# Where g and four chunks of w_out lie in SBUF, and second-product matmuls of 256 columns in four blocks

## The chip, the cores and the metric

The kernel runs on one core of a Trainium2 chip. The metric is device time in microseconds (us) of one execution. Before the change three runs took 1107.73, 1110.91 and 1111.5 us, median 1110.91 us. One execution was profiled: it took 1110.88 us, of which 1109.1 us is the span from the first to the last instruction; the remaining 1.8 us lies around it.

## The reference

Two stages, joined by a transpose. First, linear attention with an exponential feature map, for 8 batches, 8 heads, 576 positions and head dimension 64:

```python
proj = x @ w_phi                                   # for q and for k, 128 features
proj = proj - max(abs(proj), axis=-1)
phi = concat([exp(proj), exp(-proj)])              # 256 features
kv = einsum('bhsf,bhsd->bhfd', k_p, v); z = sum(k_p, axis=2)
attn = einsum('bhsf,bhfd->bhsd', q_p, kv) / (einsum('bhsf,bhf->bhs', q_p, z) + 1e-6)
```

Then a feed-forward layer on all 4608 tokens (512 model columns, 2048 hidden ones):

```python
x = attn.transpose(0, 2, 1, 3).reshape(4608, 512)
h = x @ w_in                                       # 512 -> 2048
g = 0.5 * h * (1 + erf(h / sqrt(2)))
out = g @ w_out                                    # 2048 -> 512
```

`w_in` and `w_out` are of type float64 here, handed to the kernel as 64-bit words.

## The kernel before

The feed-forward part is what the change touches. It goes through the tokens in 18 blocks of 256 (`TB`). To keep precision, each factor is split into a high and a low float32r part, and a product is three matmuls: high by high, and the two mixed ones. In `block(j, ...)`:

- The first product fills `ph`, 128 hidden columns at a time. For each of the 16 hidden chunks `f` it takes 12 matmuls: 4 chunks of the model dimension by three pairs of parts. Each has a 128x128 piece of `w_in` (tile `w_i`) as the stationary operand and 256 tokens of `xh` or `xl` as the moving one.
- ScalarE applies Gelu twice, once into `gh` (the high part, written as float32r) and once in place, and VectorE subtracts to get `gl`. Each tile holds two chunks of 256 tokens, so a unit `u` is two hidden chunks.
- The second product adds into `po`, [128, 2, 512]. For each hidden chunk it takes 6 matmuls: two halves `m` of the tokens by three pairs of parts (`gh` with both parts of `w_out`, `gl` with the high one). The stationary operand is a 128x128 piece of `gh` or `gl`, the moving one is a row of 512 columns of `w_o{f}`, the split tile of hidden chunk `f`. A block has 96 of these. Where the next thing on TensorE is a first product, the last matmul of the second product's unit is already cut in two halves of 256 columns (`cut`); in the last unit it is the one before the last.

Every matmul has its own load of the stationary operand (PEld in the profile).

The attention of the 8 batches runs interleaved with the first blocks. All operations are recorded by `op(...)` with a cost, a rank and the buffers that they read and write. `Plan.order` sorts them by rank and by when buffers come free in its own cost model, and `Plan.emit` writes them out in that order; from then on each engine follows its own fixed sequence. The tiles `gh` and `gl` have two buffers each.

Where a tile lies is settled when the program is built. `place(...)` reserves tiles in order at the start: `kvn`, the sixteen `w_o`, `gh`, `gl`, the sixteen `w_i`, `dc`, `xh`, `xl`. Addresses are bytes within a partition. In the program before, all of `w_o`, `gh`, `gl` and `w_i` start at a multiple of 256, and so do all the pieces that matmuls read of them, since the pieces are 512 or 2048 bytes apart. The moving tiles `xh` and `xl` start at 192 modulo 256, as do `kt` and `ek` of the attention; `wst` starts at 128; the buffers of `kvn` start at 128, 160, 192 and 224.

In the attention, `pk` is the projection of keys (a 128-column piece of `kt` is stationary, `wst` is moving), `pq` that of queries (`wst` is stationary), `kv` the sum over positions and `pn` the numerator (64 columns of `kvn` are stationary, `ef` is moving). Its operands are plain float32 and each of its matmuls leaves two records in the trace.

Of the kernel before, what the change touches and what calls it, by code (L numbers as in the profile page):

```python
# [10 lines left out]
F32 = mybir.dt.float32  # L11
F32R = mybir.dt.float32r
# [15 lines left out]
P = 128  # L28
# [4 lines left out]
NFC = DFF // P  # L33
SHIFT = 1e-6
KC = 9


class Buf:
# [215 lines left out]
def mm_cost(m, n):  # L254
    return (n / 2.286 + 3.0) / 1e3
# [6 lines left out]
def dve(n, psum=False, fast=False):  # L262
    return ((62 if psum else 66) + (n / 2 if fast else n)) / 960


def act(n, psum=False):
    return (n / 1.2 + (51 if psum else 93)) / 1e3
# [15 lines left out]
def fused_kernel(ctx: ExitStack, tc: tile.TileContext, qT, kT, va, w_st, w_in, w_out, out):  # L283
# [17 lines left out]
    def mm(*a, **kw):  # L301
        return tc.keep_in_program_order(nc.tensor.matmul(*a, **kw))  # L302


    def place(tag, shape, dt=F32):
        spool.tile(shape, dt, tag=tag, name=f"place_{tag}", bufs=SLOTS.get(tag, 1))

    place("kvn", [P, 4, D + 1])
    for f in range(NFC):
        place(f"w_o{f}", [P, 2, 512])  # L310
    place("gh", [P, 2, TB])
    place("gl", [P, 2, TB])
    for q in (2, 0, 3, 1):
        for c in range(NCC):
            place(f"w_i{c}_{q}", [P, 2, 512])
# [16 lines left out]
    def copy(eng, cost, dst, src, r, w, **kw):  # L332
        e = {"dve": nc.vector, "pool": nc.gpsimd}.get(eng)
        if eng == "act":
            op(eng, cost, lambda: nc.scalar.copy(out=dst(), in_=src()), r=r, w=w, **kw)  # L335
        else:
            op(eng, cost, lambda: e.tensor_copy(out=dst(), in_=src()), r=r, w=w, **kw)

    def tt(eng, cost, dst, a, b, o, r, w, **kw):
        e = {"dve": nc.vector, "pool": nc.gpsimd}[eng]  # L340
        op(eng, cost, lambda: e.tensor_tensor(out=dst(), in0=a(), in1=b(), op=o), r=r, w=w, **kw)  # L341
# [5 lines left out]
    def split_weight(src, nm, rank):  # L347
        tag = f"w_{nm}"
        raw = plan.pool(spool, tag, 1)([P, 512, 2], U32, f"raw_{nm}")
        w = plan.pool(spool, tag, 1)([P, 2, 512], F32R, f"w_{nm}")  # L350
        t = sb["ob"]([P, 512], U32, f"wt_{nm}")
        k = dict(rank=rank)
        op("sp", 0.06, lambda: nc.sync.dma_start(out=raw().bitcast(I64), in_=src), w=[raw], kb=524, **k)
        low, high = (lambda: raw()[:, :, 0]), (lambda: raw()[:, :, 1])
        v = nc.vector
        op("act", act(512) + 0.04, lambda: nc.scalar.activation(t().bitcast(F32), high().bitcast(F32), AF.Abs), r=[raw], w=[t], **k)
        op("dve", dve(512, fast=True), lambda: v.tensor_scalar(
            out=t().bitcast(F32), in0=t().bitcast(F32), scalar1=F64_MIN, scalar2=F64_MAX, op0=ALU.max, op1=ALU.min), r=[t], w=[t], **k)
        op("dve", dve(512, fast=True), lambda: v.tensor_scalar(
            out=t(), in0=t(), scalar1=3, scalar2=0x3FFFFFF8, op0=ALU.logical_shift_left, op1=ALU.bitwise_and), r=[t], w=[t], **k)  # L360
        op("dve", dve(512), lambda: v.scalar_tensor_tensor(
            out=t(), in0=low(), scalar=29, in1=t(), op0=ALU.logical_shift_right, op1=ALU.bitwise_or), r=[raw, t], w=[t], **k)
        op("dve", dve(512), lambda: v.scalar_tensor_tensor(
            out=t(), in0=high(), scalar=0xC0000000, in1=t(), op0=ALU.bitwise_and, op1=ALU.bitwise_or), r=[raw, t], w=[t], **k)
        hi = lambda: w()[:, 0, :]
        copy("act", act(512), hi, lambda: t().bitcast(F32), [t], [w], **k)
        tt("dve", dve(512), lambda: w()[:, 1, :], lambda: t().bitcast(F32), lambda: hi().bitcast(F32), ALU.subtract, [t, w], [w], **k)
        return w

    wi, wo = {}, {}  # L370

# [180 lines left out]
    def block(j, rank):  # L552
        plan.stream = "f"
        xr = sb["xr"]([P, NCC, TB], F32, f"xr_{j}")
        rb = sb["rb"]([P, NCC, TB], F32, f"rb_{j}")
        xh_all = sb["xh"]([P, NCC * TB], F32R, f"xh_{j}")
        xl_all = sb["xl"]([P, NCC * TB], F32R, f"xl_{j}")
        xh = lambda: xh_all()[:, : NCC * TB].rearrange("p (c t) -> p c t", c=NCC)
        xl = lambda: xl_all()[:, : NCC * TB].rearrange("p (c t) -> p c t", c=NCC)
        t = j * TB  # L560
        while t < (j + 1) * TB:
            b, s = divmod(t, S)
            h, s = divmod(s, HS)
            n = min(HS - s, (j + 1) * TB - t)
            o = t - j * TB
            for c in range(NCC):
                op("sp", 0.06, lambda b=b, c=c, h=h, s=s, n=n, o=o: nc.sync.dma_start(
                    out=xr()[:, c, o : o + n], in_=x_d[b][c][h]()[:, s : s + n]), r=[x_d[b][c][h]], w=[xr], kb=n * 0.512,
                   rank=rank(0) - 8)
            for i in range(2):  # L570
                op("sp", 0.06, lambda b=b, i=i, h=h, s=s, n=n, o=o: nc.sync.dma_start(
                    out=rb()[64 * i : 64 * i + 64, :, o : o + n],
                    in_=r_d[b][h]()[:, s : s + n].rearrange("(c i) t -> i c t", i=2)[i : i + 1].to_broadcast([64, NCC, n])),
                   r=[r_d[b][h]], w=[rb], kb=n * 1.024, rank=rank(0) - 8)
            t += n
        tt("dve", dve(NCC * TB), xr, xr, rb, ALU.mult, [xr, rb], [xr], rank=rank(0) - 4)
        copy("dve", dve(NCC * TB, fast=True), xh, xr, [xr], [xh_all], rank=rank(0) - 4)
        tt("dve", dve(NCC * TB), xl, xr, lambda: xh().bitcast(F32), ALU.subtract, [xr, xh_all], [xl_all], rank=rank(0) - 4)
        po = ps["po"]([P, 2, DM], F32, f"po_{j}")
        for u in range(NU):  # L580
            rk = rank(u / NU)
            ph = ps["ph"]([P, 2, TB], F32, f"ph_{j}_{u}")
            for i in range(2):

                def mm1(ph=ph, u=u, i=i):
                    ins = []
                    f = 2 * u + i
                    fs = slice(f % 4 * P, f % 4 * P + P)
                    for c in range(NCC):
                        for w, x in ((0, xh), (0, xl), (1, xh)):  # L590
                            ins.append(mm(ph()[:, i, :], lhsT=wi[c, f // 4]()[:, w, fs], rhs=x()[:, c, :], start=len(ins) == 0, stop=len(ins) == 11))
                    return ins

                op("pe", 12 * mm_cost(128, TB), mm1, r=[xh_all, xl_all] + [wi[c, u // 2] for c in range(NCC)], w=[ph], rank=rk, part="first")
            gh = sb["gh"]([P, 2, TB], F32R, f"gh_{j}_{u}")
            gl = sb["gl"]([P, 2, TB], F32R, f"gl_{j}_{u}")
            op("act", act(2 * TB, True) + 0.016, lambda gh=gh, ph=ph: nc.scalar.activation(gh(), ph(), AF.Gelu), r=[ph], w=[gh], table="gelu", rank=URGE + rk)  # L597
            op("act", act(2 * TB, True) + 0.037, lambda ph=ph: nc.scalar.activation(ph(), ph(), AF.Gelu), r=[ph], w=[ph], table="gelu", rank=URGE + rk)  # L598
            tt("dve", dve(2 * TB, True), gl, ph, lambda gh=gh: gh().bitcast(F32), ALU.subtract, [ph, gh], [gl], rank=URGE + rk, port=False)
            for i in range(2):  # L600

                def mm2(u=u, i=i, gh=gh, gl=gl):
                    ins = []
                    f = 2 * u + i
                    for m in range(2):
                        ms = slice(m * P, (m + 1) * P)
                        for n, (g, w) in enumerate(((gh, 0), (gh, 1), (gl, 0))):
                            cut = plan.then == "first" and m == 1 and n == (1 if f == NFC - 1 else 2)
                            for cs in (slice(0, DM // 2), slice(DM // 2, DM)) if cut else (slice(0, DM),):
                                ins.append(mm(po()[:, m, cs], lhsT=g()[:, i, ms], rhs=wo[f]()[:, w, cs], start=f == 0 and n == 0,  # L610
                                              stop=f == NFC - 1 and n == 2, skip_group_check=cut))
                    return ins

                op("pe", 6 * mm_cost(128, DM), mm2, r=[gh, gl, wo[2 * u + i]], w=[po], rank=rk)
        for m in range(2):
            ob = sb["ob"]([P, DM], F32, f"ob_{j}_{m}")
            copy("act", act(DM, True), ob, lambda m=m: po()[:, m], [po], [ob], rank=rank(1))
            op("sp", 0.06, lambda m=m, ob=ob: nc.sync.dma_start(out=out[j * TB + m * P : j * TB + (m + 1) * P, :], in_=ob()), r=[ob], kb=262, rank=rank(1))
# [92 lines left out]
```

## Time and profile before

| | |
|---|---|
| three runs | 1107.73, 1110.91, 1111.5 us (median 1110.91) |
| profiled execution | 1110.88 us, span 1109.1 us |
| instructions in the span | 21711 |
| VectorE busy | 475.7 us (43%) |
| ScalarE busy | 567.2 us (51%) |
| GpSimd busy | 315.9 us (28%) |
| DMA | 84.92 MB, mean 77 GB/s |

The page of the profile gives busy time by engine: PE is TensorE's matmuls, PEld its loads of stationary operands, DVE VectorE, ACT ScalarE, POOL GpSimd. A matmul's record covers its way through the array, so the records of consecutive matmuls overlap; the rate at which matmuls follow each other is read from a run of them (its length over their number), not from the mean length of a record. The chain of waits follows the work that ended last back from the last instruction and merges consecutive pieces of one engine and line. The view of stretches gives each engine's busy time, number of instructions and the granted TensorE clock between two times; it counts an instruction that reaches in from outside.

### The profile page before, as it was taken

The page shows a single profiled execution, that of the slowest core. Times are in us where ns is not written, and L with a number is a line of the kernel's source. Part 1 is how long each engine was busy: PE and PEld are TensorE (multiplying, and loading weights), DVE is VectorE, ACT ScalarE, POOL GpSimd, SP SyncE. Part 2 cuts the span into 40 slices and gives each one's busy share as a digit, 9 for nine tenths or more (in the row PEclk, how much of TensorE's full clock was granted, in tenths as well). Part 3 has the DMA queues.
Part 4 walks back from the last instruction along what each step waited for, and adds up shares of the span by engine and source line. Part 5 has one row for each costly group of instructions (what it writes and reads, how often), then busy time and mean ns, then how long its engine had stood idle before and what let it go on. Part 6 is the DMA issues. An engine that isn't in the chain of part 4 may idle for free.

```text
span 1109.1 us, 21711 instructions
## 1 busy us (share of the span) xinstructions
PE 1082.1 (98%) x9183; PEld 908.2 (82%) x9183; DVE 475.7 (43%) x743; ACT 567.2 (51%) x883; POOL 315.9 (28%) x116
## 2 busy tenths in 40 slices
PE   7879999999999999999999999999999999999998
PEld 4547868878878887888778889999999999999997
DVE  5889996364483553544645441212112112212010
ACT  5777786667777667877657642212212121212121
POOL 1330223376564574457556550000000000000000
PEclk8989999999999999999999999999999999999999
DMA  6787533124232332322411202102102012010000
GB/s 248 258 260 207 157 93 96 50 72 117 66 97 63 88 98 56 103 64 67 122 40 48 63 22 58 39 20 58 36 23 58 15 43 58 1 38 20 1 20 20
DMA packets 73938, 84.92 MB, mean 77 GB/s; under 512 B 23968, under 2 KB 60992, under 8 KB 73840
## 3 DMA queue, kind: packets, MB, share of 16 engines
q1 hardware_dynamic: 73840, 83.52, 25.3%
q8 instruction: 72, 1.18, 0.5%
q14 instruction: 26, 0.21, 0.1%
HBM read 64.32 MB, written 19.17 MB: 75 GB/s over the span
## 4 chain that ended last, share of the span: by engine, by line
PE 86%; DVE 6%; ACT 4%; DMA 2%; issue 1%; POOL 1%; ACTq 0%; SPq 0%; POOLq 0%; DVEq 0%
PE po L302 35%; PE ph L302 34%; PE pn L302 6%; PE kv L302 5%; PE pq L302 3%; PE pk L302 3%; ACT ek L430 1%; DVE mx L425 1%; DVE ek L341 1%; ACT ef L479 1%; DMA x_d<-xo 1%; PE spin L302 1%; DMA d_d<-xo 1%; DMA kt<-in_kT_dram 1%; ACT L597 0%
## 5 line engine op out<-in xcount | busy, mean ns | idle before, releaser
L302 PE MATMUL ph<-xh,w_i 128*128 128x256 f32 x2304 | 418.5, 279 | 0.0
L302 PEld LDWEIGHTS ph<-xh,w_i 128*128 128x128 f32 x2304 | 357.2, 188 | 7.9 <-issue 6.3
L302 PE MATMUL po<-w_o,gh 128*128 128x512 f32 (+1 forms) x1168 | 363.6, 394 | 0.0
L302 PE MATMUL ph<-xl,w_i 128*128 128x256 f32 x1152 | 319.2, 277 | 0.0
L341 DVE TENSOR_TENSOR gl<-ph,gh 128x512 fp32r<-128x512 f32 x144 | 99.2, 689 | 415.8 <-ACT ph L598 413.4
L302 PEld LDWEIGHTS po<-w_o,gh 128*128 128x128 f32 x1168 | 211.3, 188 | 49.7 <-issue 6.0
L597 ACT ACTIVATE gh<-ph 128x512 fp32r<-128x512 f32 x144 | 86.1, 598 | 298.9 <-PE ph L302 298.2
L302 PE MATMUL po<-w_o,gl 128*128 128x512 f32 (+1 forms) x647 | 226.1, 367 | 1.7 <-DVE gl L341 1.7
L508 POOL PARTITION_ALL_REDUCE db<-un x48 | 174.9, 3645 | 154.7 <-DVE un L505 122.0
L302 PEld LDWEIGHTS ph<-xl,w_i 128*128 128x128 f32 x1152 | 216.7, 188 | 0.7
L473 POOL PARTITION_ALL_REDUCE mb<-pc x64 | 142.9, 2232 | 187.8 <-ACT pc L335 145.5
L302 PEld LDWEIGHTS po<-w_o,gl 128*128 128x128 f32 x647 | 121.9, 188 | 27.8 <-DVE gl L341 2.1
L302 PEld LDWEIGHTS kv<-vt,ek 128*64 128x64 f32 (+1 forms) x2560 | 84.1, 139 | 28.0 <-issue 14.5
L302 PE MATMUL pn<-ef,kvn 128*64 128x288 f32 (+1 forms) x512 | 97.4, 423 | 6.3 <-ACT xo L335 6.3
L302 PE MATMUL kv<-vt,ek 128*64 128x65 f32 (+1 forms) x2560 | 93.7, 226 | 2.9 <-ACT ek L430 2.2
L430 ACT ACTIVATE ek<-ek 128x1024 f32<-128x1024 f32 (+1 forms) x96 | 80.8, 843 | 26.8 <-DVE ek L341 25.6
L479 ACT ACTIVATE ef<-pc 128x576 f32<-128x576 f32 x128 | 81.6, 678 | 22.7 <-DVE pc L341 22.1
L598 ACT ACTIVATE ph<-ph 128x512 f32<-128x512 f32 x144 | 85.6, 594 | 0.0
L341 DVE TENSOR_TENSOR pc<-pc,mb 128x576 f32<-128x576 f32 x64 | 53.7, 840 | 52.5 <-POOL mb L473 52.3
L302 PEld LDWEIGHTS pn<-ef,kvn 128*64 128x64 f32 (+1 forms) x512 | 39.5, 138 | 38.0 <-ACT xo L335 12.0
L597 ACT ACT_TABLE_LOAD x47 | 60.3, 1283 | 8.9 <-PE ph L302 8.1
L425 DVE TENSOR_REDUCE mx<-pk 128x8 f32<-128x1024 f32 (+1 forms) x48 | 45.6, 954 | 44.2 <-PE pk L302 44.2
(41 smaller groups left out, 672.0 us busy)
## 6 DMA issues: line engine op xcount, KB each, us to landing
vt<-in_va_dram SPq DMA_DIRECT2D x16, 585.0 KB
qt<-in_qT_dram SPq DMA_DIRECT2D x64, 144.0 KB
kt<-in_kT_dram SPq DMA_DIRECT2D x16, 576.0 KB
out_dram<-ob SPq DMA_DIRECT2D x36, 256.0 KB
raw_i<-in_w_in_dram SPq DMA_DIRECT2D x16, 512.0 KB
raw_o<-in_w_out_dram SPq DMA_DIRECT2D x16, 512.0 KB
x_d<-xo SPq DMA_DIRECT2D x48, 144.0 KB
x_d<-xo SPq DMA_DIRECT2D x32, 72.0 KB
```

The costliest lines, as they stand in the source:

```text
L302: return tc.keep_in_program_order(nc.tensor.matmul(*a, **kw))
L341: op(eng, cost, lambda: e.tensor_tensor(out=dst(), in0=a(), in1=b(), op=o), r=r, w=w, **kw)
L425: op("dve", dve(256 * n, True), lambda xs=xs, mx=mx: nc.vector.tensor_reduce(out=mx(), in_=xs(), axis=AX.X, op=ALU.max, apply_absolute_val ...
L430: op("act", act(256 * n), lambda e=e, s=s: nc.scalar.activation(e[s](), e[1](), AF.Exp, scale=1.0 - 2.0 * s), r=[e[1]], w=[e[s]], table="e ...
L473: op("pool", 2.2, lambda mb=mb, pc=pc: nc.gpsimd.partition_all_reduce(mb(), pc(), P, bass_isa.ReduceOp.absmax), r=[pc], w=[mb], port="max" ...
L479: op("act", act(2 * HS), lambda ef=ef, pc=pc, s=s: nc.scalar.activation(ef()[:, s], pc(), AF.Exp, scale=1.0 - 2.0 * s), r=[pc], w=[ef], ta ...
L508: op("pool", 3.7, lambda db=db, un=un: nc.gpsimd.partition_all_reduce(db(), un(), P, bass_isa.ReduceOp.add), r=[un], w=[db], port="add", * ...
L597: op("act", act(2 * TB, True) + 0.016, lambda gh=gh, ph=ph: nc.scalar.activation(gh(), ph(), AF.Gelu), r=[ph], w=[gh], table="gelu", rank= ...
L598: op("act", act(2 * TB, True) + 0.037, lambda ph=ph: nc.scalar.activation(ph(), ph(), AF.Gelu), r=[ph], w=[ph], table="gelu", rank=URGE + rk)
```

## The change

It has three parts, all in `split_weight`, `block` and the reservations.

1. `gh` and `gl` become rows of 576 elements (`GW`) in place of 512. From block 10 on, the 512 elements in use start at element 0, 16, 32 or 48, that is, 0, 64, 128 or 192 bytes: block 10 at 0, 11 at 64, 12 at 128, 13 at 192, and 14 to 17 in the same order. Blocks 0 to 9 stay at 0.
2. The tiles of hidden chunks 8 to 11 of `w_out` become 1088 elements wide, and their contents start at element 48, 192 bytes in, in all blocks. The two places add 2048 bytes a partition, and every tile behind them moves by a multiple of 256.
3. In blocks 10 to 13 all matmuls of the second product are cut in two halves of 256 columns, apart from the last pair of parts of the last hidden chunk (two matmuls a block). `start` is set on the first half alone, since that clears the bank that both halves share.

No cost or rank handed to the planner changes. On ScalarE, VectorE, GpSimd and SyncE the same instructions stand in the same sequence as before. On TensorE only the cuts differ: 7583 matmuls in the program in place of 7227.

The start of block 10's second product on TensorE, before (`po_10` is the block's sum; then the moving tile, hidden chunk 0 and then 1 of `w_out`, and the stationary tile of unit 0):

```order
L302 MATMUL po_10_8334<-w_o0_544,gh_10_0_8316 128x512 x2
L302 MATMUL po_10_8334<-w_o0_544,gl_10_0_8320 128x512
L302 MATMUL po_10_8334<-w_o0_544,gh_10_0_8316 128x512 x2
L302 MATMUL po_10_8334<-w_o0_544,gl_10_0_8320 128x512
L302 MATMUL po_10_8334<-w_o1_637,gh_10_0_8316 128x512 x2
L302 MATMUL po_10_8334<-w_o1_637,gl_10_0_8320 128x512
```

The same place on TensorE with the change:

```order
L304 MATMUL po_10_8334<-w_o0_544,gh_10_0_8316 128x256 x4
L304 MATMUL po_10_8334<-w_o0_544,gl_10_0_8320 128x256 x2
L304 MATMUL po_10_8334<-w_o0_544,gh_10_0_8316 128x256 x4
L304 MATMUL po_10_8334<-w_o0_544,gl_10_0_8320 128x256 x2
L304 MATMUL po_10_8334<-w_o1_637,gh_10_0_8316 128x256 x4
L304 MATMUL po_10_8334<-w_o1_637,gl_10_0_8320 128x256 x2
```

Each matmul of 512 columns has become two of 256; nothing stands elsewhere than it did.

The end of the same second product on TensorE, before (unit 7, hidden chunks 14 and 15):

```order
L302 MATMUL po_10_8334<-w_o14_2011,gh_10_7_8605 128x512 x2
L302 MATMUL po_10_8334<-w_o14_2011,gl_10_7_8619 128x512
L302 MATMUL po_10_8334<-w_o15_2110,gh_10_7_8605 128x512 x2
L302 MATMUL po_10_8334<-w_o15_2110,gl_10_7_8619 128x512
L302 MATMUL po_10_8334<-w_o15_2110,gh_10_7_8605 128x512
L302 MATMUL po_10_8334<-w_o15_2110,gh_10_7_8605 128x256 x2
L302 MATMUL po_10_8334<-w_o15_2110,gl_10_7_8619 128x512
```

And with the change:

```order
L304 MATMUL po_10_8334<-w_o14_2011,gh_10_7_8680 128x256 x4
L304 MATMUL po_10_8334<-w_o14_2011,gl_10_7_8699 128x256 x2
L304 MATMUL po_10_8334<-w_o15_2110,gh_10_7_8680 128x256 x4
L304 MATMUL po_10_8334<-w_o15_2110,gl_10_7_8699 128x512
L304 MATMUL po_10_8334<-w_o15_2110,gh_10_7_8680 128x256 x4
L304 MATMUL po_10_8334<-w_o15_2110,gl_10_7_8699 128x512
```

The matmul that was cut already stays as it was, and the two with `gl` of the last chunk keep their 512 columns.

The diff, cut to its core:

```diff
+GW = 2 * TB + 64
+AT192 = (8, 9, 10, 11)
...
     for f in range(NFC):
-        place(f"w_o{f}", [P, 2, 512])
-    place("gh", [P, 2, TB])
-    place("gl", [P, 2, TB])
+        place(f"w_o{f}", [P, 1088 if f in AT192 else 1024])
+    place("gh", [P, GW])
+    place("gl", [P, GW])
...
-        w = plan.pool(spool, tag, 1)([P, 2, 512], F32R, f"w_{nm}")
+        off = 48 if nm in [f"o{f}" for f in AT192] else 0
+        w_all = plan.pool(spool, tag, 1)([P, 1024 + (64 if off else 0)], F32R, f"w_{nm}")
+        w = lambda: w_all()[:, off : off + 1024].rearrange("p (a b) -> p a b", a=2)
...
-            gh = sb["gh"]([P, 2, TB], F32R, f"gh_{j}_{u}")
-            gl = sb["gl"]([P, 2, TB], F32R, f"gl_{j}_{u}")
+            gh_all = sb["gh"]([P, GW], F32R, f"gh_{j}_{u}")
+            gl_all = sb["gl"]([P, GW], F32R, f"gl_{j}_{u}")
+            off = 16 * ((j - 10) % 4) if j >= 10 else 0
+            gh, gl = (lambda t=t, off=off: t()[:, off : off + 2 * TB].rearrange("p (i t) -> p i t", i=2) for t in (gh_all, gl_all))
...
-                            cut = plan.then == "first" and m == 1 and n == (1 if f == NFC - 1 else 2)
+                            halves = 10 <= j < 14
+                            cut = (halves and not (f == NFC - 1 and n == 2)) or plan.then == "first" and m == 1 and n == (1 if f == NFC - 1 else 2)
                             for cs in (slice(0, DM // 2), slice(DM // 2, DM)) if cut else (slice(0, DM),):
-                                ins.append(mm(po()[:, m, cs], lhsT=g()[:, i, ms], rhs=wo[f]()[:, w, cs], start=f == 0 and n == 0,
-                                              stop=f == NFC - 1 and n == 2, skip_group_check=cut))
+                                ins.append(mm(po()[:, m, cs], lhsT=g()[:, i, ms], rhs=wo[f][0]()[:, w, cs], start=f == 0 and n == 0 and cs.start == 0,
+                                              stop=f == NFC - 1 and n == 2, skip_group_check=cut or halves))
```

More of the change, by code (lines that the diff above doesn't have):

```diff
@@ L365, in split_weight @@
         hi = lambda: w()[:, 0, :]
-        copy("act", act(512), hi, lambda: t().bitcast(F32), [t], [w], **k)
-        tt("dve", dve(512), lambda: w()[:, 1, :], lambda: t().bitcast(F32), lambda: hi().bitcast(F32), ALU.subtract, [t, w], [w], **k)
-        return w
+        copy("act", act(512), hi, lambda: t().bitcast(F32), [t], [w_all], **k)
+        tt("dve", dve(512), lambda: w()[:, 1, :], lambda: t().bitcast(F32), lambda: hi().bitcast(F32), ALU.subtract, [t, w_all], [w_all], **k)
+        return w, w_all
     wi, wo = {}, {}
@@ L590, in mm1 @@
                         for w, x in ((0, xh), (0, xl), (1, xh)):
-                            ins.append(mm(ph()[:, i, :], lhsT=wi[c, f // 4]()[:, w, fs], rhs=x()[:, c, :], start=len(ins) == 0, stop=len(ins) == 11))
+                            ins.append(mm(ph()[:, i, :], lhsT=wi[c, f // 4][0]()[:, w, fs], rhs=x()[:, c, :], start=len(ins) == 0, stop=len(ins) == 11))
                     return ins
-                op("pe", 12 * mm_cost(128, TB), mm1, r=[xh_all, xl_all] + [wi[c, u // 2] for c in range(NCC)], w=[ph], rank=rk, part="first")
-            gh = sb["gh"]([P, 2, TB], F32R, f"gh_{j}_{u}")
-            gl = sb["gl"]([P, 2, TB], F32R, f"gl_{j}_{u}")
-            op("act", act(2 * TB, True) + 0.016, lambda gh=gh, ph=ph: nc.scalar.activation(gh(), ph(), AF.Gelu), r=[ph], w=[gh], table="gelu", rank=URGE + rk)
+                op("pe", 12 * mm_cost(128, TB), mm1, r=[xh_all, xl_all] + [wi[c, u // 2][1] for c in range(NCC)], w=[ph], rank=rk, part="first")
+            gh_all = sb["gh"]([P, GW], F32R, f"gh_{j}_{u}")
+            gl_all = sb["gl"]([P, GW], F32R, f"gl_{j}_{u}")
+            off = 16 * ((j - 10) % 4) if j >= 10 else 0
+            gh, gl = (lambda t=t, off=off: t()[:, off : off + 2 * TB].rearrange("p (i t) -> p i t", i=2) for t in (gh_all, gl_all))
+            op("act", act(2 * TB, True) + 0.016, lambda gh=gh, ph=ph: nc.scalar.activation(gh(), ph(), AF.Gelu), r=[ph], w=[gh_all], table="gelu", rank=URGE + rk)
             op("act", act(2 * TB, True) + 0.037, lambda ph=ph: nc.scalar.activation(ph(), ph(), AF.Gelu), r=[ph], w=[ph], table="gelu", rank=URGE + rk)
-            tt("dve", dve(2 * TB, True), gl, ph, lambda gh=gh: gh().bitcast(F32), ALU.subtract, [ph, gh], [gl], rank=URGE + rk, port=False)
+            tt("dve", dve(2 * TB, True), gl, ph, lambda gh=gh: gh().bitcast(F32), ALU.subtract, [ph, gh_all], [gl_all], rank=URGE + rk, port=False)
             for i in range(2):
@@ L607, in mm2 @@
                         for n, (g, w) in enumerate(((gh, 0), (gh, 1), (gl, 0))):
-                            cut = plan.then == "first" and m == 1 and n == (1 if f == NFC - 1 else 2)
+                            halves = 10 <= j < 14
+                            cut = (halves and not (f == NFC - 1 and n == 2)) or plan.then == "first" and m == 1 and n == (1 if f == NFC - 1 else 2)
                             for cs in (slice(0, DM // 2), slice(DM // 2, DM)) if cut else (slice(0, DM),):
-                                ins.append(mm(po()[:, m, cs], lhsT=g()[:, i, ms], rhs=wo[f]()[:, w, cs], start=f == 0 and n == 0,
-                                              stop=f == NFC - 1 and n == 2, skip_group_check=cut))
+                                ins.append(mm(po()[:, m, cs], lhsT=g()[:, i, ms], rhs=wo[f][0]()[:, w, cs], start=f == 0 and n == 0 and cs.start == 0,
+                                              stop=f == NFC - 1 and n == 2, skip_group_check=cut or halves))
                     return ins
-                op("pe", 6 * mm_cost(128, DM), mm2, r=[gh, gl, wo[2 * u + i]], w=[po], rank=rk)
+                op("pe", 6 * mm_cost(128, DM), mm2, r=[gh_all, gl_all, wo[2 * u + i][1]], w=[po], rank=rk)
         for m in range(2):
```

## The prediction

> **What bounds the kernel now.** I begin with the page: engines, granted clock, chain.
>
> ```profile
> PE 1082.1 (98%) x9183; PEld 908.2 (82%) x9183; DVE 475.7 (43%) x743; ACT 567.2 (51%) x883; POOL 315.9 (28%) x116
> ...
> PEclk8989999999999999999999999999999999999999
> ...
> PE 86%; DVE 6%; ACT 4%; DMA 2%; issue 1%; POOL 1%; ACTq 0%; SPq 0%; POOLq 0%; DVEq 0%
> ```
>
> TensorE is busy throughout and holds 86% of the chain, at nearly full granted clock after the first slices. Its busy share alone doesn't say that it streams without gaps, because records overlap. So next comes the view of stretches: blocks 8 and 9, blocks 10 to 13, blocks 14 to 17.
>
> ```profile
> core 0: us, PE busy (x) PEld busy (x) DVE busy (x) ACT busy (x) POOL busy (x), PEclk, DMA share, GB/s
> 664.60:752.00 87.40, 87.40 (x588) 80.17 (x587) 17.34 (x24) 19.56 (x36) 0.00 (x0) 1.00 0.14 37
> 752.00:926.90 174.90, 174.90 (x1174) 160.43 (x1173) 34.03 (x45) 39.12 (x72) 0.00 (x0) 1.00 0.14 37
> 926.90:1104.80 177.90, 177.84 (x1184) 162.48 (x1183) 28.23 (x39) 39.13 (x73) 0.00 (x0) 1.00 0.07 22
> ```
>
> From 664.6 us on the attention is over (POOL does nothing), the clock is 1.00, and DVE and ACT work about a fifth of the time. Blocks 10 to 17 take 174.9 + 177.9 = 352.8 us. All the halving and all the new places of `gh` and `gl` fall here; only the four shifted chunks of `w_out` reach into earlier blocks. The view of waits for 752 to 1104.8 us tells who waits for whom:
>
> ```profile
> DVE gl L341 <- ACT ph L598: 280.5, 58, 7.5
> ACT gh L597 <- PE ph L302: 226.8, 64, 7.1
> ACT ob L335 <- PE po L302: 49.2, 9, 5.8
> ```
>
> The long waits are those of DVE and ACT for work that begins with TensorE; TensorE itself has no row in that answer. What is left is its own pace, which the chain shows for block 17 (start, length, engine, tile, number of matmuls):
>
> ```profile
> 1061.06 5.47 PE ph L302 x48
> 1066.53 5.46 PE po L302 x25
> ...
> 1093.83 5.46 PE ph L302 x48
> 1099.29 5.47 PE po L302 x24
> ```
>
> These four rows carry the argument. A `ph` run is two units of the first product: 48 matmuls of 256 columns, 12288 columns in all. A `po` run is two units of the second: 24 products of 512 columns, again 12288, one of which is already cut in two where the row says x25. All take 5.46 or 5.47 us. So TensorE pays for columns, 5.46 us / 12288 = 0.444 ns each, and it makes no visible difference whether they come as 24, 25 or 48 matmuls. In a `ph` run a matmul follows every 5.46 / 48 = 0.1138 us, each with its own load of a stationary operand.
>
> **The change part by part.** The sum is made against the profiled execution, 1110.88 us (span 1109.1 and 1.8 around it), 0.03 below the median of the three runs.
>
> *Halving in blocks 10 to 13.* It adds 7583 - 7227 = 356 matmuls and as many loads, and no column. The second product of these blocks is 4 x 4 = 16 `po` runs, each of which becomes what a `ph` run is today. The nearest rows price a run at 5.46 to 5.47 us in either form, so the difference is between -0.01 and +0.01 us a run, -0.2 to +0.2 us over 16. These rows include the change from one product to the other at the run's edge. The far bound comes from single records in the view by form, for 752 to 1104.8 us:
>
> ```profile
> L302 PE MATMUL ph<-xh,w_i 128*128 128x256 f32 x1024 | 181.2, 277 | 0.0
> ...
> L302 PE MATMUL po<-w_o,gl 128*128 128x256 f32 x62 | 12.3, 280 | 0.0
> ```
>
> A half matmul of the second product has a record 3 ns longer than one of the first. If every added one cost that, it would be 356 x 3 ns = 1.1 us. A gain below -0.2 us I exclude, as no column goes. I take 0: the runs measure the pace itself, the records only a length that overlaps.
>
> By the Trainium skill's page "TensorE: Matmul & The Clock Gate", section "Back-to-back issue gap", a warm matmul takes its columns at 2.4 GHz and a fixed 2.5 ns, so the same 356 would cost an estimated 0.9 us and a matmul of 256 columns would take 109 ns. The runs here show 114 ns, and a cost in proportion to columns without a fixed part that can be seen; the measurement decides.
>
> *What hides the added loads.* The loads run ahead beside the matmuls. Their room shrinks from one load in 227 ns to one in 114 ns. Two stretches, a `po` run and the `ph` run behind it, show what that looks like today:
>
> ```profile
> 771.35:776.81 5.46, 5.46 (x28) 4.55 (x27) 0.69 (x1) 1.09 (x2) 0.00 (x0) 1.00 0.00 0
> 776.81:782.27 5.46, 5.46 (x50) 5.46 (x49) 0.69 (x1) 1.09 (x2) 0.00 (x0) 1.00 0.00 0
> ```
>
> In the second the load lane is busy all 5.46 us and the matmuls keep their pace. So a load takes no more than 114 ns of it, from an address at a multiple of 256. What it takes at other addresses is the open question of the change.
>
> *`gh` and `gl` at 64, 128 and 192.* They are stationary operands, so the loads feel it (blocks 11 to 13 halved, 15 to 17 whole). The trace of before has loads from other addresses, in the attention:
>
> ```profile
> L302 PEld LDWEIGHTS po<-w_o,gh 128*128 128x128 f32 x1168 | 211.3, 188 | 49.7 <-issue 6.0 <-ACT kvn L335 0.8 <-ACT gh L597 0.4
> ...
> L302 PEld LDWEIGHTS pk<-wst,kt 64*128 64x128 f32 x576 | 36.7, 191 | 15.0 <-issue 7.1 <-ACT pc L335 5.1 <-DVE wt_i L359 0.4
> L302 PEld LDWEIGHTS pn<-ef,kvn 128*64 128x64 f32 x384 | 23.3, 136 | 17.0 <-issue 2.8 <-ACT xo L335 1.2
> L302 PEld LDWEIGHTS pq<-qt,wst 64*128 64x128 f32 x256 | 19.5, 186 | 23.5 <-issue 12.2 <-ACT pc L335 4.3 <-DVE ek L341 2.4
> ```
>
> With 128 columns a load takes 188 ns at 0 (`gh`), 191 at 192 (`kt`) and 186 at 128 (`wst`): no trend, though the last two are plain float32 from 64 partitions. And the chain around 600 us has a run of such loads at 192:
>
> ```profile
> 604.66 0.97 PE pn L302 x8
> ...
> 611.47 1.09 PE pk L302 x16
> ```
>
> Sixteen records of `pk`, each with its load of 128 columns of `kt`, follow each other in 1.09 us, 68 ns each, well under 114. So I take 0 for 128 and 192, and for 64, of which no row has a load of 128 columns, also 0, by its neighbours. Blocks 15 to 17 need no such argument: there a load has 227 ns.
>
> *Chunks 8 to 11 of `w_out` at 192.* They are moving operands. In a `ph` run the moving operand, `xh` or `xl`, lies at 192 today, in a `po` run `w_o` lies at 0, and both take 5.46 us. Price 0. They are also written there, once, by ACT and DVE:
>
> ```profile
> L335 ACT CAST w_o<-wt_o x16: 604/618/624, 42.9 to 176.6; 128x512 fp32r<-128x512 f32 x16
> L341 DVE TENSOR_TENSOR w_o<-wt_o,w_o x16: 624/684/1382, 43.5 to 177.3; 128x512 fp32r<-128x512 f32 x16
> ```
>
> Were these writes half as long again, it would be 4 x (0.31 + 0.34) = 2.6 us spread over two engines before 178 us. I take 0: the `ek` tiles lie at 192, too, and these are the same engines.
>
> *Writes of `gh` and `gl` at the new places.* What hides a longer write is the next unit's first product. The timeline around 758 us, and the chain's start of the run that needs the result:
>
> ```profile
> 758.24 0.60 ACT L598 ACTIVATE ph<-ph 128x512 f32<-128x512 f32 x1
> 758.87 0.69 DVE L341 TENSOR_TENSOR gl<-ph,gh 128x512 fp32r<-128x512 f32 x1 [6.82 <-ACT ph L598]
> ...
> 760.43 5.46 PE po L302 x25
> ```
>
> `gl` is done at 759.56, 0.87 us ahead of the run. ACT's two passes and the subtraction together would have to lose that before TensorE waits. Nothing queues up behind them, as both engines are idle most of the time.
>
> Sum: 1110.88 + 0 + 0 + 0 = 1110.9 us, which I round to 1111.
>
> **The rivals.**
>
> *S, slower: the load becomes the bound in the halved blocks.* Mechanism: a load of 512 bytes from 64, 128 or 192 touches three stretches of 256 bytes, not two, and takes half as long again. The price from rows: 128 columns 188 ns, 64 columns 136, so some 50 ns per 64 columns and about 100 ns for a load's own time (an estimate from these two). Half as long again is 150 ns. The rival decides from 114 ns on, and only where 188 halves a block follow each other: (150 - 114) x 188 = 6.8 us a block, 20.3 us for blocks 11 to 13, total 1131. If 64 alone does it, block 11 pays, total 1117.7. For it: the full load lane in a `ph` run, and a cover of only 14 ns. Against it: the same length of loads at 128 and 192, and the 68 ns of `pk`. Chance 0.08, evenly between the two. By the same page, section "LDWEIGHTS (loading the stationary operand)", a load of 128 columns takes an estimated 107 ns. By that the cover would be 7 ns, not 14, and S would begin sooner; no run here shows that time by itself.
>
> *F, faster: the pace of 0.444 ns a column is itself a clash of two reads at the same place modulo 256, and goes where `gh` is moved.* The price: the fastest long run in these rows is `pn` above, 8 records of 288 columns in 0.97 us, 0.421 ns a column, 5.2% less. Blocks 11 to 13 and 15 to 17 have 6 x 4 `po` runs, 131 us, of which 5.2% is 6.8 us: 1104. For it: two tables of addresses are just what would change it. Against it: a `ph` run reads its operands at 192 and 0 and is as slow as a `po` run at 0 and 0; and such a clash should hurt a `ph` run twice as much, as it has twice the loads to a column. Chance 0.06.
>
> *N, the change doesn't do what it says*, for instance because the halves are fused or the offsets fall away in the build. It would give 1110.9 as well, with no x48 in the rows of `po`; it adds nothing to either side.
>
> **How the numbers follow.** About 0.3%, 3.3 us, is what a measurement of this kernel can tell from no change; the three runs lie 3.8 us apart. The forecast of no change has 0.86, S 0.08, F 0.06. Of the forecast's share I give 0.02 to a measurement that comes out slower by chance or by the far bound of 1.1 us, and 0.01 to one that comes out faster. So: faster 0.07, same 0.83, slower 0.10. The range goes from 1107 (the lowest run) to 1116: the 1.1 us of the halving and the same scatter upwards, with a little of S where it is weak. It leaves out most of S and all of F, some 0.15.
>
> **What would show it.** Right: in blocks 10 to 13 the chain has `po` rows of x46 to x48 at 5.46 or 5.47 us, with the load lane busy throughout; in 14 to 17 the rows stay as they are; 752 to 1104.8 us holds the same work. The forecast is wrong if `po` rows of block 10 are longer than 5.47 us (halving costs), if those of 11 to 13 are longer than block 10's (S), or if those of 15 to 17 are shorter than block 14's (F). A different time before 664 us would be the shifted chunks of `w_out`, or nothing of this change.

## The result, and the profile after

The changed kernel took 1116.85 us (median of 7 runs, 1113.77 to 1118.32), the kernel before 1110.52 us beside it (7 runs, 1107.73 to 1111.58): ratio 1.0058, 95% interval 1.004 to 1.0075. That is 6.3 us slower; I had forecast no change, 1111 us, with a range up to 1116. The profiled execution took 1118.32 us, its span is 1116.5 us.

The page of the changed kernel, engines and chain:

```profile
PE 1086.8 (97%) x9539; PEld 925.9 (83%) x9539; DVE 476.7 (43%) x743; ACT 567.0 (51%) x883; POOL 316.2 (28%) x116
...
PE 86%; DVE 5%; ACT 5%; DMA 2%; issue 1%; POOL 1%; SPq 0%; ACTq 0%; POOLq 0%
```

There are 356 more matmuls and loads, as counted, and the chain is TensorE's as before. The view of stretches, cut where blocks 8, 10 and 14 begin and where the second product of block 17 ends:

```profile
665.60:753.70 88.10, 88.10 (x588) 80.63 (x587) 17.43 (x25) 19.57 (x36) 0.00 (x0) 1.00 0.14 37
753.70:932.00 178.30, 178.30 (x1522) 177.58 (x1521) 34.00 (x45) 39.13 (x72) 0.00 (x0) 1.00 0.14 36
932.00:1112.20 180.20, 180.17 (x1193) 164.03 (x1191) 28.14 (x38) 39.12 (x72) 0.00 (x0) 1.00 0.07 21
```

Beside 87.4, 174.9 and 177.9 us before, these are 0.7, 3.4 and 2.3 us more: 6.4 us, as much as the medians differ by. (The two profiled executions are 7.4 us apart; the other 1.0 us lies ahead of block 8.) The granted clock is 1.00 in all three stretches. It isn't the halved blocks alone. The chain says which runs became longer; first block 10 (operands of the second product at 0 and 0 in the first two `po` rows, `w_out` at 192 in the third):

```profile
762.10 5.74 PE po L304 x48
767.84 5.46 PE ph L304 x48
773.30 5.74 PE po L304 x48
779.04 5.46 PE ph L304 x48
784.50 5.44 PE po L304 x48
789.94 5.44 PE ph L304 x48
```

Block 10 has `gh` and `gl` at 0, as before. Its halved runs took 5.74 us, not 5.46; but the run whose chunks of `w_out` lie at 192 took 5.44. Then block 14, nothing halved, `gh` and `gl` at 0:

```profile
951.28 5.46 PE po L304 x25
956.74 5.46 PE ph L304 x48
962.20 5.59 PE po L304 x25
967.79 5.65 PE ph L304 x48
```

Here the same chunks at 192 take 5.59 us, and the first product behind them 5.65, though nothing about that product has changed. And block 15, `gh` and `gl` at 64:

```profile
984.40 5.59 PE po L304 x25
990.00 5.66 PE ph L304 x48
995.65 5.61 PE po L304 x25
1001.26 5.46 PE ph L304 x48
```

In the view by form for 753.7 to 932 us the loads' records are as long as ever, whatever their place:

```profile
L304 PEld LDWEIGHTS ph<-xh,w_i 128*128 128x128 f32 x513 | 79.3, 188 | 0.0
L304 PEld LDWEIGHTS po<-w_o,gh 128*128 128x128 f32 x505 | 68.9, 189 | 0.4
```

### The profile page after: what moved, and what is told of

The parts are those of the page before. It is cut to its first block, busy times and chain, and to the rows that moved or that the text cites. A ratio compares the mean times of both kernels' runs of the same rounds, so it can differ in the third digit from the quotient of the medians.

```text
span 1116.5 us, 22423 instructions
## 1 busy us (share of the span) xinstructions
PE 1086.8 (97%) x9539; PEld 925.9 (83%) x9539; DVE 476.7 (43%) x743; ACT 567.0 (51%) x883; POOL 316.2 (28%) x116
## 4 chain that ended last, share of the span: by engine, by line
PE 86%; DVE 5%; ACT 5%; DMA 2%; issue 1%; POOL 1%; SPq 0%; ACTq 0%; POOLq 0%
PE po L304 35%; PE ph L304 34%; PE pn L304 6%; PE kv L304 6%; PE pq L304 3%; PE pk L304 3%; DMA x_d<-xo 1%; ACT ek L434 1%; DVE mx L429 1%; DVE ek L343 1%; ACT ef L483 1%; PE spin L304 0%; ACT L603 0%; DVE pc L343 0%; ACT pc L337 0%
## 5 line engine op out<-in xcount | busy, mean ns | idle before, releaser
L304 PEld LDWEIGHTS po<-w_o,gh 128*128 128x128 f32 x1420 | 233.5, 189 | 42.3 <-issue 6.0
L304 PEld LDWEIGHTS po<-w_o,gl 128*128 128x128 f32 x751 | 133.2, 189 | 22.9 <-DVE gl L343 2.1
```

## The experiments

All start from the kernel before, with the wider rows of `gh` and `gl`. The places are set by tables: pads ahead of a tile (in elements of 4 bytes), an offset of `gh` and `gl` by block, and the list of blocks with halves. A table that isn't shown is empty or 0. The frame of them:

```diff
+    def pad(nm, n):
+        if n:
+            place(nm, [P, n])
     for f in range(NFC):
+        pad(f"pad_o{f}", WO_PAD.get(f, 0))
         place(f"w_o{f}", [P, 1024])
+    pad("pad_o16", WO_PAD.get(16, 0))
...
+            off = G_AT(j)
...
+                            halves = j in HALVES
```

Pads of one table add up to a multiple of 256 bytes, so that what lies behind keeps its place modulo 256. `X_PAD` stands in the same way ahead of `xh` (what is left to 64 elements behind `xl`), `WI_PAD` ahead of the pieces of `w_in`, and `X_AT` is an offset of `xh` and `xl` by block. In the texts below, P, D, S and T are steps of one theory: the two operands' places together set the pace (P), only by their difference modulo 256 (D), with two paces at some differences, kept from run to run (S), and decided by differences across the change of product (T). H says that a slow pace is a state handed on. L is rival S of the prediction, a longer load; the S of these texts is another theory. A is a rival of D: one address alone sets the pace.

**The parts alone, and the first product moved.**

```diff
+HALVES = (10, 11, 12, 13)
```

> Only the halving in blocks 10 to 13; gh, gl and w_out stay at 0 modulo 256. Theory P (the pair of places of moving and stationary operand modulo 256, together with the width of the matmul, sets the pace): all second products of these blocks are then 256 wide with both operands at 0, which took 5.74 us a run of 48 in block 10 of the changed kernel against 5.46; so 16 x 0.28 = 4.5 us slower, about 1115, with the ph runs at 5.46. Theory H (a slow pace is a state that one run hands to the next, whatever the places): the ph runs behind the slow po runs are slow as well (5.65), 6 to 8 us slower. Theory L (the one of the prediction: only a longer load from 64, 128 or 192 costs): no change, 1110 to 1111, po runs of 48 at 5.46.

```diff
+WO_PAD = {8: 48, 12: 16}
```

> Only chunks 8 to 11 of w_out at 192 modulo 256, in all blocks; no halving, gh and gl at 0. P: the run of these chunks (512 wide, 192 and 0) goes from 5.46 to 5.59 us in each of 18 blocks and nothing else changes, so 2.3 us slower, about 1113. H: the ph run behind it is slow too (5.65), 0.32 us a block, 5.8 us in 18 blocks, about 1116. L: no change.

```diff
+G_AT = lambda j: 16 * ((j - 10) % 4) if j >= 10 else 0
```

> Only gh and gl at 0, 64, 128 and 192 in blocks 10 to 13 and again in 14 to 17; no halving, w_out at 0. P: the po runs of blocks 11, 12, 13, 15, 16 and 17 take 5.50 to 5.60 us, those of 10 and 14 5.46, so about 6 x 4 x 0.11 = 2.6 us slower, 1113, and blocks 11 to 13 repeat 15 to 17. H: besides, some ph runs behind them take 5.65, up to 4 us more. L: no change, since a load has 227 ns here.

```diff
     place("dc", [P, HS // 16])
+    pad("pad_x", 16)
     place("xh", [P, XW], F32R)
     place("xl", [P, XW], F32R)
+    pad("pad_y", 48)
```

> Nothing of the change; instead xh and xl, the moving operands of the first product, are put at 0 modulo 256 in place of 192. P: the first product is then 256 wide with both operands at 0, the slow pair of block 10, 120 ns a matmul in place of 114: 3456 x 6 ns = 21 us slower, about 1131, in all 18 blocks. H: no change beyond 3 us, as the places only disturb and do not set the pace. L: no change, since the stationary operands stay at 0.

| kernel | median us | ratio to before, 95% interval | blocks 8-9, 10-13, 14-17, us |
|---|---|---|---|
| before | 1108.97 | | 87.5, 174.9, 177.8 |
| halves_only | 1114.66 | 1.0051 (1.0038 to 1.0064) | 87.5, 179.5, 178.0 |
| w_out_only | 1112.93 | 1.0038 (1.0026 to 1.005) | 88.1, 176.2, 179.0 |
| g_only | 1113.72 | 1.0042 (1.003 to 1.0055) | 87.5, 177.2, 180.3 |
| x_at_0 | 1130.89 | 1.0189 (1.017 to 1.0207) | 90.0, 180.0, 182.8 |

The last column is worked out from the trace as above (start of block 8, 10 and 14, end of the last matmul). It repeats to 0.1 us where kernels agree, while the start of block 8 moves by some us between profiles; so it tells more than the medians. Each part alone costs 4 to 6 us. L has fallen: the halves cost 4.6 us with all loads at multiples of 256, and `g_only` costs as much in 14 to 17 as in 10 to 13 without a halved matmul. In the chain of `halves_only` all twelve whole `po` runs of blocks 10 to 13 stand at 5.74 or 5.75 us, and the first products between them at 5.46, not slow as H has it:

```profile
760.27 5.74 PE po L310 x48
766.01 5.46 PE ph L310 x48
771.47 5.74 PE po L310 x48
```

`x_at_0` hits P's number, 1131 (four runs, 1125.87 to 1131.91). It touches nothing that the change touches, and its first product runs at the pace of the halved second one, since it is now 256 wide with both operands at 0:

```profile
775.99 5.76 PE ph L310 x48
781.75 5.47 PE po L310 x25
787.22 5.76 PE ph L310 x48
```

In `w_out_only` the median is what P said, but the chain is H's: in each block from 8 on the run of the moved chunks takes 5.59 us and hands a slow first product on, 5.65 us. Neither foresaw both. In `g_only`, too, the median is P's (1113), but some first products take H's 5.65 us.

```profile
681.11 5.46 PE po L310 x25
686.57 5.46 PE ph L310 x48
692.03 5.59 PE po L310 x25
697.62 5.65 PE ph L310 x48
```

**Maps of all pairs.**

```diff
+HALVES = (10, 11, 12, 13)
+G_AT = lambda j: 16 * ((j - 10) % 4) if j >= 10 else 0
+WO_PAD = {2: 16, 6: 16, 10: 16, 14: 16}
```

> w_out by runs of the second product at 0 (chunks 0, 1, 14, 15), 64 (2 to 5), 128 (6 to 9) and 192 (10 to 13); gh and gl at 0, 64, 128, 192 in blocks 10 to 13 (256 wide) and again in 14 to 17 (512 wide): all 16 pairs at both widths. Theory D (only the difference, moving less stationary modulo 256, counts, with the width): 512 wide 227 to 228 ns a matmul at difference 0, 228 to 232 at 64, 232 at 128, 233 at 192, also for the eight pairs with w_out at 64 and 128 that no run has shown; 256 wide 119 to 120 at 0, 113 or 116 at 64, 118.5 at 128, 113 or 118 at 192. Theory A (only one of the two addresses counts): all four pairs of one moving place, or of one stationary place, have one pace, 231 to 233 or 227 at 512 wide. Time in all 1113 to 1120 by either.

```diff
+HALVES = (14, 15, 16, 17)
+G_AT = lambda j: 16 * ((9 - j) % 4) if j >= 10 else 0
+WO_PAD = {2: 48, 6: 48, 10: 48, 14: 48}
```

> As map_1 with the order of the places turned round: w_out at 0 (chunks 0, 1, 14, 15), 192 (2 to 5), 128 (6 to 9), 64 (10 to 13); gh and gl at 192, 128, 64, 0 in blocks 10 to 13 (512 wide) and in 14 to 17 (256 wide). D without any memory of the run before: each pair has the same pace as in map_1, to 1 ns. D with two states (H): pairs at differences 0 and 128 agree to 1 ns, and some at 64 and 192 differ between the two runs by 4 to 5 ns at 256 wide, as another run stands ahead of them.

```diff
+X_AT = lambda j: 16 * (j % 4) if j >= 10 else 48
+X_PAD = 16
+WI_PAD = {0: 16, 3: 16, 1: 16, 4: 16}
```

> The same map for the first product, 256 wide: xh and xl at 128, 192, 0, 64 in blocks 10 to 13 and 14 to 17 and at 192 before, w_in at 0, 64, 128, 192 by quarter; second product untouched. D: difference 0 takes 120 ns a matmul, 128 takes 118.5, 64 and 192 take 113.3 or 116 to 118. A (moving place alone): x at 192 is fast with all four places of w_in. In all D gives slower than before by about half of what x_at_0 cost in blocks 0 to 17, some 8 to 12 us, so about 1118 to 1122; A gives 5 us or less in blocks 10 to 17 alone.

```diff
+G_AT = lambda j: (4, 8, 12, 20, 36, 56, 60, 64)[j - 10] if j >= 10 else 0
```

> gh and gl at 16, 32, 48, 80, 144, 224, 240 and 256 bytes in blocks 10 to 17, w_out at 0, nothing halved, so differences of 240, 224, 208, 176, 112, 32, 16 and 0. If the period is 256 bytes, block 17 is at 226.7 ns a matmul. If only whole steps of 64 bytes count, 16, 32 and 48 behave like 0 or like 192 (226.7 or 233.3), 80 like 64 or 128, 144 like 128 or 192. If each 16 bytes count, the pace changes gradually between them. In all 2 to 6 us slower than before.

One run each: 1121.67, 1119.64, 1120.62 and 1113.48 us. From the traces I take the mean distance between the starts of consecutive matmuls, in the second half of each stretch with one pair, from 680 us on. Ordered by the difference, moving less stationary operand modulo 256, all pairs, both products and all four maps fall together, apart from single short stretches, which differ by up to 5 ns:

| difference | 512 wide, ns | 256 wide, ns |
|---|---|---|
| 0 | 226.7 (a few stretches 230 to 232, behind a change of pair) | 120.0, all pairs, both products |
| 16 | 226.7 | |
| 32 | 233.3 | |
| 64 | 228.8 to 229.6; in `g_only`, with 0 and 192, also 233.3 | 117.8; 113.3 in a few |
| 112, 176 | 233.3, 232.0 | |
| 128 | 232 to 234 | 118.2 to 120.0 |
| 192 | 232.8 to 234.0 | 113.3 or 117.8 |
| 208, 224, 240 | 233.3 | |

Here D stands and A falls: a moving place of 192 is at 226.7 or at 233.3 according to its partner. Block 17 of `map_fine`, 256 bytes on, is back at 226.7, and so is the difference 16, though not 32. That only whole steps of 64 bytes count doesn't fit: 32 takes 233.3 ns, while 0 takes 226.7 and 64 in these maps 228.8 to 229.6. In the chain of `map_fine`, block 10 (difference 240) and block 16 (16):

```profile
759.27 5.60 PE po L310 x25
...
```

```profile
1036.22 5.45 PE po L310 x25
```

The kernel before stood at the best of both columns: difference 0 at 512 wide, 192 (at the faster of two paces) at 256 wide. The largest loss of a matmul and its load is nearly the same at both widths, 233.3 - 226.7 = 6.6 ns and 120.0 - 113.3 = 6.7 ns, though at different differences; at 256 wide there are twice as many matmuls to lose it. And D isn't all: at 256 wide and difference 192 there are two paces.

**Two paces, and what keeps them.**

```diff
+HALVES = range(NBLK)
+WO_PAD = {0: 48, 16: 16}
```

> All 16 chunks of w_out at 192, gh and gl at 0, and the second product 256 wide in all 18 blocks: 1605 more matmuls than before and every operand away from where it was fast, but at the pair (192, 0) that the first product has. D: fast state throughout, 5.44 us a run in both products as in the third and fourth run of block 10 of the changed kernel, 0.02 us a run less than before, 1107 to 1109 against 1109 to 1111. L, or any fixed cost for a matmul: 1605 x 2.5 ns = 4 us slower. H with the slow state caught somewhere in the attention and handed on: 5.65 us a run, up to 0.2 us x 8 x 18 = 29 us slower.

It took 1124.25 us, ratio 1.0135 (1.0111 to 1.0158). D without memory misses by 15 us. From 646 us on both products run at 117.8 ns to the end, the slow one of the two paces, not once at 113.3:

```profile
727.52 5.65 PE po L310 x48
733.17 5.65 PE ph L310 x48
738.83 5.65 PE po L310 x48
```

```diff
+G_AT = lambda j: 48
+WO_PAD = {0: 48, 16: 16}
```

> All of w_out at 192 modulo 256 and gh and gl at 192 in all blocks, nothing halved. D (the difference counts): the second product is back at difference 0, 512 wide, 226.7 ns a matmul, 5.46 us a run, as before; time as before, 1108 to 1111. If each address counted by itself: 233 ns as in w_out_only or 232 as in g_only, 10 to 16 us slower.

It took 1119.49 us, ratio 1.0082 (1.0065 to 1.01): a miss for D, though its own number held. The second product is back at its pace; the first product, untouched, has its runs of 48 at 5.65 us, 117.8 ns a matmul:

```profile
763.77 5.47 PE po L310 x25
769.25 5.65 PE ph L310 x48
774.90 5.47 PE po L310 x25
```

Not all of it is slow: the 36 matmuls behind a block's last unit take 4.08 or 4.09 us, 113.3 ns each, at the same places modulo 256. The second product ahead of them ends in a whole matmul; those ahead of the slow runs end in two halves. Whether that decides was not tried. From block 8 on this kernel loses 6.5 us; the rest of the difference lies ahead of it.

The next two also cut the last pair of parts (`cut = halves or ...`, `stop` on the second half).

```diff
+HALVES = range(NBLK)
+G_AT = lambda j: 48 if j == 12 else 0
+WO_PAD = {0: 48, 16: 16}
```

> As w_out_192_halves_all (second product 256 wide in all blocks, w_out at 192, gh and gl at 0, difference 192), but gh and gl at 192 in block 12, so that this one block has difference 0, the slowest at 256 wide; the last pair of parts is cut as well. Theory S (at difference 192 and 256 wide a run keeps the pace of the run ahead, 113.3 or 117.8 ns): blocks 8 to 11 at 117.8, block 12's second product at 120.0, and its first product and all of blocks 13 to 17 at 113.3; about 8 us faster than w_out_192_halves_all, 1116. Without such a state: blocks 13 to 17 at 117.8 as before block 12, 1124 to 1125.

It took 1124.19 us, ratio 1.0137 (1.0117 to 1.0156). The block at difference 0 did not bring the fast pace back; the slow one outlived it. Chain of blocks 12 and 13:

```profile
861.77 5.76 PE po L310 x48
867.53 5.66 PE ph L310 x48
...
896.01 5.65 PE po L310 x48
901.66 5.65 PE ph L310 x48
```

```diff
+HALVES = range(8, NBLK)
+G_AT = lambda j: 48 if j < 8 else 0
+WO_PAD = {0: 48, 16: 16}
```

> w_out at 192; gh and gl at 192 and 512 wide in blocks 0 to 7 (difference 0), at 0 and 256 wide from block 8 on (difference 192), all pairs of parts cut. S: block 7 leaves the first product fast, and from there both products stay at 113.3 ns, 5.44 us a run against 5.46 before: 1.5 us faster than before, 1107 to 1109. If the state doesn't hold: 117.8 ns from some block on, up to 16 us slower, 1125.

It took 1109.94 us (11 runs), ratio 1.0005 (0.9994 to 1.0015). From its second product of block 8 on it has the very places of `w_out_192_halves_all`, and in blocks 8 to 11 the very program of `slow_then_reset`. Now the fast pace lasts to the end, 438.2 us for blocks 8 to 17 against 440.2 before; blocks 8 to 11 take 174.2 us, against 180.9 in `slow_then_reset`. The first product just ahead, 36 matmuls, took 4.08 us here, 113.3 ns each, and 4.24 us there, 117.8 ns each:

```profile
669.94 4.08 PE ph L310 x36
674.02 5.44 PE po L310 x48
679.47 5.44 PE ph L310 x48
684.90 5.44 PE po L310 x48
```

So S holds in that a pace once taken is kept, for over 400 us, where all differences within a product are 192. The 2 us don't show in the median. Blocks 0 to 7 have the places of `moved_together`, which can cost them there; I didn't separate that from the start's scatter.

```diff
+G_AT = lambda j: 48
+WO_PAD = {0: 48, 16: 16}
+X_PAD = 48
+WI_PAD = {2: 48, 4: 16}
```

> As moved_together (w_out, gh and gl at 192 modulo 256, nothing halved), and w_in at 192 and xh and xl at 128 as well: all four operands of both products are moved by 192 against before, so that every difference is as before, within a product and from one product to the next. Theory T (what counts is differences alone, also at the change from one product to the other, and this decides which of its two paces a ph run takes): ph runs at 113.3 and po runs at 226.7 ns from 665 us on, 5.46 us a run each, as before; 1108 to 1111. If moved_together was slow because of the place 192 itself: ph runs at 117.8 there, 1116 to 1120 as moved_together, or more.

It took 1108.15 us (12 runs) beside 1109.57, ratio 0.9993 (0.9981 to 1.0005), with both products at the pace of before:

```profile
762.43 5.46 PE ph L310 x48
767.88 5.46 PE po L310 x25
```

From block 8 to the end it takes 440.2 us, as before. All four operands are elsewhere than before and the time is the same, while the two of the second product moved and the two of the first left behind (`moved_together`) had ratio 1.0082, some 9 us. T holds for this one shift: with every difference as before, within a product and from one to the next, the places themselves don't matter. Which difference across the change of product threw `moved_together` into the slow pace, no run shows by itself.

## Why the prediction was wrong

- **What bounds the kernel** was read rightly: TensorE's own pace, 0.444 ns a column, nobody waited for. All 6.4 us came out of that pace.
- **"I take 0" for the halving failed**, and with it the bounds of 0.2 and 1.1 us: 4.6 us in `halves_only`. The step read a `ph` run of 48 and a `po` run of 24 as the same thing in another cut. They differ in the difference of their operands' places, 192 and 0. At 256 wide, 0 is the slowest pair (5.74 us), at 512 wide the best. No row of before had a run of halves with both operands at 0.
- **"Price 0" for chunks 8 to 11 at 192 failed** for the same reason. That `ph` at 192 and `po` at 0 both take 5.46 us was taken to mean that the place doesn't matter. It meant that both sat at a good point. The chunks cost 0.13 us a run and 0.19 in the run behind them. The trace of before had a warning: of the last two first products ahead of block 8, 24 matmuls each at unchanged places, one goes at 113.3 ns a matmul (from 655.0 us) and one at 117.8 (from 658.9 us).
- **"Also 0" for `gh` and `gl` at 64, 128, 192 failed.** I argued that a load in a whole matmul has 227 ns and hides; but up to 6.6 ns a matmul are lost at 512 wide too, and 4.5 ns a matmul in some first products behind them (5.65 us a run): 2.3 to 2.5 us per four blocks.
- In the change the parts don't add up, 3.4 us in blocks 10 to 13 against 4.6 + 1.3 + 2.3 alone, as some halved runs come to a pair at a fast pace: the 5.44 us of block 10, where the chunks at 192 meet `gh` and `gl` at 0.
- **Rival S** gave the right sign and, with 1117.7, nearly the time, but by luck, from a mechanism that the runs don't show: the loads' records stay at 188 to 189 ns, and block 10, which S left out, has halved runs of 5.74 us. **Rival F** had the dependence, on the two reads' places modulo 256, and the wrong sign: it took the pace of before for the disturbed one. Its objection, that `ph` and `po` are equally slow, was the trap. The Trainium skill's 2.5 ns for a warm matmul ("TensorE: Matmul & The Clock Gate", "Back-to-back issue gap", there for an isolated one) would have made the halves cost an estimated 0.9 us. The runs show 4.6 us in `halves_only`, and 0 to 6.7 ns a matmul over the fastest pace, by the pair.
- The check named for S, block 10 against 11 to 13, and for halving, `po` rows of block 10 over 5.47 us, did tell at first sight which step failed.

## What to carry to other kernels

Where matmuls follow each other without gaps, give moving and stationary operands places whose difference modulo 256 bytes is one that was measured to be fast for that width, and look at it again whenever a tile ahead of them grows or a matmul is cut. Two kinds of matmul with one pace don't show that the places don't matter: both can be at a good point, as here. When an operand must move, move all of them by the same amount; the runs show this for one shift, 192 bytes.

## What the runs showed of the hardware

- The pace of back-to-back float32r matmuls with a load each depends on the difference of the two operands' places modulo 256 bytes: 226.7 or up to 233.3 ns at 512 columns, 113.3 or up to 120.0 ns at 256. The fast window at 512 is narrow: 0 and 16, not 32 or 240.
- Which difference is fast depends on the width: 0 (with 16) is the best at 512, 226.7 ns, and with 120.0 ns the slowest at 256.
- At 256 columns and difference 192 there are two steady paces, 113.3 and 117.8 ns. With the same places from block 8 on, blocks 8 to 17 took 438.2 us in one (`fast_handed_on`) and 455.2 in the other (`w_out_192_halves_all`, where two matmuls a block stay whole), by what had run ahead; blocks 8 to 11 took 174.2 and, with the very same program, 180.9 us (`slow_then_reset`).
- That the reads of load and moving operand meet in the same part of the memory would fit the dependence on the difference and the like loss per matmul at both widths. It is argued, not shown: no run took the loads away. What throws a run into the one pace or the other isn't settled either; `g_only` and `moved_together` have fast and slow `ph` runs behind the same pair.
